# One fixed program order for TensorE, VectorE and ScalarE of a DeltaNet and Fourier-mixing kernel, with the third group begun earlier and two kinds of small products on four PE tiles

## Chip, cores and metric

The kernel runs on one core of one Trainium2 chip. The metric is device time in microseconds (us) of one execution, as the median of several. Spans in the profile are some 2 us shorter than the timed values.

## The reference, cut to what matters

```python
# DeltaNet: 4 batches, 8 heads, 768 positions, head size 48
k_n = k / (norm(k) + 1e-6)
for t in range(768):
    y[t]  = q[t] @ state                       # state is 48 x 48 for each head
    v_old = state^T @ k_n[t]
    state = state + beta[t] * outer(k_n[t], v[t] - v_old)
x = y as (4, 768, 384)
# Fourier mixing and MLP
u  = x + real(fft(fft(x, axis=1), axis=2))
un = (u - mean(u)) / sqrt(var(u) + 1e-6)
out = u + relu(un @ w1) @ w2                   # w1: 384 x 1536, w2: 1536 x 384
```

## The kernel before

The scan over positions is done in chunks of 64, so a batch is 12 **steps** and the whole scan is 48 (steps 0 to 47). Each step multiplies with a small inverse matrix that depends only on the keys. These inverses are made for two quads of four chunks at a time, which is called a **group** (six in all): VectorE inverts blocks of 32 (`invert`, tiles X and A), TensorE joins them (`merge`, tile pj) and ScalarE copies the result to `wt`. Once a batch is scanned, it is mixed (`fourier`) and goes through the MLP (tiles ph and po) in three groups of 256 rows.

Instructions that go through the wrapper keep the program's order on their engine while a flag is set. All others may be moved on their engine by the scheduler that builds the program. (PE is TensorE in the profile, DVE is VectorE, ACT is ScalarE.) In the kernel before, the flag is set in batch 0 and during the preparation of the third group's keys, and is off otherwise:

```python
    strict = [False]

    class Ordered:
        def __init__(self, engine):
            self.engine = engine

        def __getattr__(self, name):
            def call(*args, **kwargs):
                ins = getattr(self.engine, name)(*args, **kwargs)
                if strict[0]:
                    tc.keep_in_program_order(ins)
                return ins
            return call

    dve, act, pe = Ordered(nc.vector), Ordered(nc.scalar), Ordered(nc.tensor)
```

One step of the scan is a chain over three engines:

```python
    def chain(m):
        # ... cut: buffers; pc is a PSUM tile
        for j in range(2):                                   # pc <- st, KQT: 16 products in the profile
            for hh, e in ((0, 0), (1, 1), (0, 1), (1, 0)):
                pr = slice(64 * e, 64 * e + D)
                mm(pk[64 * hh:64 * hh + 64, e, j], KQT[pr, c, j, hh, 0, :], st[pr, hh, D * j:D * j + D], True)
        dve.tensor_tensor(U.rearrange(ue, e=2), V4[:, c].rearrange(ue, e=2), pk, op=ALU.subtract)
        yield
        for u in range(4):                                   # pc <- U, wt: 16 products in the profile
            for hh in range(2):
                pr = slice(64 * hh, 64 * hh + 64)
                mm(pu[pr, u], wt[pr, c, u], U[pr, u], True)
        act.activation(U, pu, ACT.Copy)
        yield
        # ... cut: loads
        for j in range(2):                                   # pc <- U, kp: 16 products in the profile
            for hh, e in ((0, 0), (1, 1), (0, 1), (1, 0)):
                pr = slice(64 * hh, 64 * hh + 64)
                mm(pS[64 * e:64 * e + 64, hh, D * j:D * j + D], kp[pr, c, 2 * j + e, :], U[pr, 2 * j + e], True)
        dve.tensor_tensor(nst, st, pS, op=ALU.add)           # the next step's state
        # ... cut: outputs (py) are left to later
        yield
```

In batch 0 the program itself says what stands between the steps' products. Afterwards it only issues preparation (`pre`) and mixing with MLP (`side`) at a rate per third of a step, and the scheduler places them:

```python
    strict[0] = True
    # ... cut: batch 0, steps 0 to 11, with the merges of groups 0 and 1 and the first weight's conversion
    run(rest)
    strict[0] = False

    PRE, SIDE = 2.4, (0.0, 1.5, 2.2, 2.2)
    pre, side, due = ahead(2), iter(()), [0.0, 0.0]
    for m in range(NCH, STEPS):
        b, n = divmod(m, NCH)
        g = m // (2 * QT)
        if m % (2 * QT) == 0:
            run(pre)                                   # a group's merge is complete before its first step
            pre = ahead(g + 1) if g + 1 < NG else iter(())
            due = [0.0, 0.0]
        for i, _ in enumerate(chain(m)):
            # ... cut: outputs; at a batch's first step, side = second(b - 1): mixing, then MLP
            if m > NCH or i > 0:
                due[0] += 4.6 if g == 1 else PRE
                due[1] += SIDE[b]
            # ... cut: advance side and pre as they fall due
```

## Time and profile before

| | before |
|---|---|
| time, median of 3 runs | 786.97 us (786.54 to 793.07) |
| span of the profiled execution | 784.7 us |
| TensorE marked busy | 699.9 us |
| mean granted clock | 0.97 |
| first product of step 12 (batch 1 begins) | 142.3 us |
| first ph (the MLP begins) | 180.3 us |
| first product of step 17 | 255.8 us |

Steps are found in the trace by their first product, `pc<-st,KQT`; a program that counts these gives the times of the table. The prediction below shows the main lines of this profile. Two more rows of its page are needed later: VectorE's busy tenths and the granted clock, in 40 slices of the span.

```profile
DVE  2699766575992598245961119783111146100000
PEclk9999999989998999699999999899999999999999
```

### The profile page before, as it was taken

What the parts mean: (1) busy time and instruction counts of PE and PEld (TensorE: products, weight loads), DVE (VectorE), ACT (ScalarE), POOL (GpSimd) and SP (SyncE); (2) the same over time, 40 slices, a digit from 0 to 9 for tenths busy, and PEclk for the clock granted to TensorE, in tenths of its full rate; (3) what the DMA queues carried; (4) which work ended last, traced back from release to release, by engine and by line L of the source; (5) the groups of instructions that cost most, each with busy time, mean ns of one, the idle gap of its engine ahead of it and who ended that gap; (6) DMA issues with size and microseconds to landing.
All of it is one profiled execution on the core that took longest, in us unless ns stands there. A gap on an engine that the chain in (4) does not pass through costs nothing.

```text
span 784.7 us, 17842 instructions
## 1 busy us (share of the span) xinstructions
PE 699.9 (89%) x7640; PEld 513.0 (65%) x7640; DVE 379.4 (48%) x952; ACT 260.0 (33%) x634; POOL 58.7 (7%) x83
## 2 busy tenths in 40 slices
PE   5852799989988997999989998999999989999997
PEld 4531687867656765786666775776767666677684
DVE  2699766575992598245961119783111146100000
ACT  3741354227436404532152540315312121021120
POOL 8020000010000001010100001010000010100000
PEclk9999999989998999699999999899999999999999
DMA  8651033225320212001202101001000000000000
GB/s 189 163 113 31 7 85 57 46 74 123 87 69 9 38 32 43 16 10 25 50 6 42 32 2 42 1 1 32 12 12 11 12 11 1 20 1 20 11 11 20
DMA packets 82447, 30.75 MB, mean 39 GB/s; under 512 B 77392, under 2 KB 78928, under 8 KB 82368
## 3 DMA queue, kind: packets, MB, share of 16 engines
q1 hardware_dynamic: 78224, 22.31, 13.8%
q0 software_dynamic: 1968, 6.91, 2.7%
q8 instruction: 60, 0.98, 0.5%
q10 hardware_dynamic: 2176, 0.39, 0.3%
q14 instruction: 19, 0.16, 0.1%
HBM read 24.87 MB, written 4.72 MB: 38 GB/s over the span
## 4 chain that ended last, share of the span: by engine, by line
PE 48%; DVE 10%; ACT 5%; issue 3%; DMA 0%; SPq 0%; POOL 0%; POOLq 0%; DVEq 0%; ACTq 0%
PE ph L131 20%; PE po L131 15%; DVE X L131 3%; PE pc L131 3%; DVE A L131 2%; PE pf L131 2%; PE pj L131 2%; ACT A L131 2%; PE pb L131 2%; ACT wt L131 1%; PE pg L131 1%; PE py L131 1%; DVE sm L131 1%; DVE x L131 1%; PE pt L131 1%
## 5 line engine op out<-in xcount | busy, mean ns | idle before, releaser
L131 PE MATMUL ph<-unT,w 128*128 128x256 f32 x864 | 213.8, 395 | 4.5 <-ACT unT L131 2.0
L131 PE MATMUL po<-w,hT 128*128 128x384 f32 x576 | 202.2, 498 | 1.7 <-ACT KQT L131 0.7
L131 PEld LDWEIGHTS ph<-unT,w 128*128 128x128 f32 x864 | 160.3, 193 | 33.7 <-ACT hT L131 3.7
L131 PEld LDWEIGHTS po<-w,hT 128*128 128x128 f32 x576 | 105.7, 191 | 68.2 <-issue 1.5
L131 ACT ACTIVATE hT<-ph 128x256 f32<-128x256 f32 x144 | 54.9, 383 | 179.6 <-PE ph L131 179.3
L131 DVE TENSOR_TENSOR x<-x,po 128x384 f32<-128x384 f32 x24 | 13.2, 552 | 112.5 <-PE po L131 112.4
L131 ACT ACTIVATE U<-pc 128x192 f32<-128x192 f32 x48 | 15.9, 331 | 110.0 <-PE pc L131 98.4
L131 ACT ACTIVATE KQT<-pt 128x256 f32<-128x256 f32 (+1 forms) x82 | 32.0, 419 | 44.9 <-PE pt L131 44.3
L131 PEld LDWEIGHTS pc<-U,wt 64*64 64x64 f32 x768 | 34.0, 163 | 19.7 <-issue 10.3
L131 PE MATMUL pg<-KQT 48*64 48x64 f32 (+1 forms) x1024 | 41.7, 309 | 5.5 <-ACT KQT L131 4.4
L131 PEld LDWEIGHTS pg<-KQT 48*64 48x64 f32 x1024 | 32.1, 178 | 20.4 <-ACT KQT L131 11.2
L131 PE MATMUL pc<-U,wt 64*64 64x48 f32 x768 | 41.2, 253 | 4.7 <-DVE U L131 2.1
L131 DVE TENSOR_TENSOR st<-st,pc 128x192 f32<-128x192 f32 x44 | 15.3, 347 | 61.0 <-PE pc L131 56.8
L131 DVE TENSOR_TENSOR U<-V,pc 128x192 f32<-128x192 f32 x48 | 16.8, 350 | 53.1 <-PE pc L131 52.9
L131 DVE TENSOR_TENSOR A<-X 128x30 f32<-128x30 f32 (+14 forms) x120 | 41.0, 342 | 2.9
L131 DVE TENSOR_TENSOR X<-X,A 128x30 f32<-128x30 f32 (+14 forms) x120 | 39.5, 329 | 2.9
L131 DVE TENSOR_TENSOR x<-x,pb 128x193 f32<-128x193 f32 (+1 forms) x96 | 26.4, 346 | 23.1 <-PE pb L131 23.1
L716 POOL DMA_INDIRECT out_dram<-x,rows_hi x12 | 12.3, 1024 | 335.9 <-DVE x L131 179.9
L131 PE MATMUL pt<-pack,kp 128*128 128x128 f32 x96 | 24.4, 349 | 10.3 <-DMA pack<-k_pack 4.8
L131 PE MATMUL pt<-pack,qp 128*128 128x128 f32 x96 | 23.4, 341 | 11.0 <-DMA qp<-in_q_dram 11.0
L131 PE MATMUL pj<-Z,A 32*64 32x64 f32 x320 | 15.0, 257 | 19.9 <-DVE Z L131 19.6
L131 ACT ACTIVATE A<-pg 128x256 f32<-128x256 f32 (+1 forms) x72 | 25.4, 378 | 21.7 <-PE pg L131 16.6
(125 smaller groups left out, 840.2 us busy)
## 6 DMA issues: line engine op xcount, KB each, us to landing
qp<-in_q_dram SPq DMA_DIRECT2D x96, 48.0 KB, 2.4
V<-in_v_dram SPq DMA_DIRECT2D x96, 48.0 KB, 2.4
kp<-in_k_dram SPq DMA_DIRECT2D x80, 48.0 KB, 2.5
w<-in_moe_w_ch_dram SPq DMA_DIRECT2D x8, 384.0 KB, 3.2
w<-in_moe_w_ch_dram POOLq DMA_DIRECT2D x6, 384.0 KB, 6.4
x<-in_moe_w_ch_dram SPq DMA_DIRECT2D x6, 384.0 KB, 3.7
x<-in_moe_w_ch_dram POOLq DMA_DIRECT2D x4, 384.0 KB, 9.2
out_dram<-x SPq DMA_DIRECT2D x8, 192.0 KB, 2.0
```

Source lines behind the costliest of these rows:

```text
L131: ins = getattr(self.engine, name)(*args, **kwargs)
L716: nc.gpsimd.indirect_dma_start(out=out.rearrange("b s m -> (b s) m"), out_offset=bass.IndirectOffsetOnAxis(ap=rows_hi[:, i:i + 1], axis=0) ...
```

## The change

The intent is to decide the whole order by hand. The flag that keeps program order is never cleared any more, on TensorE, VectorE and ScalarE. The MLP of all four batches becomes one stream of pieces (`mlps`) that are put between the products of the steps, at a fixed rate. The third group's inverse and merge stand between and behind steps 12 to 15, placed by hand. The two next quads' keys are prepared in batch 0. The adds of the mixing are done for two rows of tiles at once (six instructions in place of eight). The products `pc<-U,wt` read one half of the partitions and write the other in half of the cases, so that they use four PE tiles and not two (a PE tile is counted here as one combination of half read and half written; 16 such products took 1.09 us before and take 0.68 us after, both early in the run); so do the joining products pj of groups 2 to 5 (`crossed`), whose results then need twice as many, smaller copies by ScalarE.

```diff
     strict[0] = True
     # batch 0 ...
+    next_keys = keys(4, 5)
+    key_work = {(7, 0): 2, (8, 2): 3, (9, 0): 1, (10, 2): 2, (11, 0): 1, (11, 1): 2, (11, 2): 1}
+    first_mixing = fourier(0)
     run(rest)
-    strict[0] = False
-    PRE, SIDE = 2.4, (0.0, 1.5, 2.2, 2.2)
+    # steps 12 to 15 with the first mixing, the second weight and the third inverse, in an order by hand
+    for i in range(9):
+        next(channels)
+        advance(w, 3)
+        if i % 2 == 1:
+            advance(steps)
+        else:
+            advance(between)
+    run(w)
+    i = 0
+    while advance(inverse, 2):
+        next(channels)
+        i += 1
+        advance(between if i > 3 else steps)
+    run(between, steps)
+    for _ in merge(2):
+        next(channels)
+    pre, mixing, due = ahead(2), iter(()), [0.0] * 3
+    for m in range(NCH + QT, STEPS):
+        for i, _ in enumerate(chain(m)):
+            due = [d + r for d, r in zip(due, (1.05 if m < 2 * NCH + 4 else 2.05, 4.0, 1.1))]
+            # advance channels (MLP), pre and mixing as they fall due
```
```diff
-        for u in range(4):
-            for hh in range(2):
-                pr = slice(64 * hh, 64 * hh + 64)
-                mm(pu[pr, u], wt[pr, c, u], U[pr, u], True)
+        for j in range(2):
+            for e in range(2):
+                for hh in range(2):
+                    pr = slice(64 * (hh ^ e), 64 * (hh ^ e) + 64)
+                    mm(pu[64 * hh:64 * hh + 64, e, j], wt[pr, c, 2 * j + e], U[pr, 2 * j + e], True)
```
```diff
+            add(x[T][:, :, 0:HD + 1], pb[:, None, 0:HD + 1].broadcast_to([128, 2, HD + 1]), ALU.add)
+            add(x[T][:, :, HD + 1:DM], pb[:, None, HD - 1:0:-1].broadcast_to([128, 2, HD - 1]), ALU.add)
             for t, op in enumerate((ALU.subtract, ALU.add)):
-                add(x[T][:, t, 0:HD + 1], pb[:, 0:HD + 1], ALU.add)
-                add(x[T][:, t, HD + 1:DM], pb[:, HD - 1:0:-1], ALU.add)
```

Cut: the first merge in halves with the first state early, values and lengths stored for the crossed layout, the first mixing's folds begun in step 10.

## The prediction

> **What bounds the kernel now.** I read the page first, then the busy time by stretches of the span, then the timeline of single stretches.
>
> ```profile
> span 784.7 us, 17842 instructions
> PE 699.9 (89%) x7640; PEld 513.0 (65%) x7640; DVE 379.4 (48%) x952; ACT 260.0 (33%) x634; POOL 58.7 (7%) x83
> PE   5852799989988997999989998999999989999997
> L131 PE MATMUL ph<-unT,w 128*128 128x256 f32 x864 | 213.8, 395 | 4.5 <-ACT unT L131 2.0
> L131 PE MATMUL po<-w,hT 128*128 128x384 f32 x576 | 202.2, 498 | 1.7 <-ACT KQT L131 0.7
> ```
>
> TensorE is marked busy 89%, but that does not mean 89% used[...]. So I priced the work by its spacing where TensorE runs back to back. In the chain that ended last the end of the kernel reads:
>
> ```profile
> 683.35 15.82 PE ph L131 x72
> 700.18 15.63 PE po L131 x48
> ```
>
> One group of 256 rows of the MLP costs 31 us; the 12 groups cost 12 x 31.2 = 375 us and nothing in the change makes them cheaper. The timeline gives the small products, early (before any MLP) and late (between MLP products):
>
> ```profile
> 102.08 0.68 PE L131 MATMUL pc<-st,KQT 48*64 48x48 f32 x16
> 104.26 1.11 PE L131 MATMUL pj<-w 32*64 32x64 f32 x16
> 112.18 1.09 PE L131 MATMUL pc<-U,wt 64*64 64x48 f32 x16
> ...
> 423.92 1.15 PE L131 MATMUL pj<-Z,A 32*64 32x64 f32 x32
> 436.51 0.49 PE L131 MATMUL pc<-U,wt 64*64 64x48 f32 x10
> 589.24 0.45 PE L131 MATMUL pc<-st,KQT 48*64 48x48 f32 x16
> ```
>
> Two things are to be seen. The same 16 products take 0.68 us early and 0.45 late[...]. And the products with wt, and pj, take 1.6 times what the products with KQT take, although they are as many: they use two PE tiles, the others four. Late prices per instruction, from start to next start: pc 17 ns, pc with wt 30, py 21.5, pj 34, pg 28, pt 110, pf 100, pb 165, ptr 100, ph 216, po 325. Now the stretches:
>
> ```profile
> 0.00:88.30 88.30, 47.95 (x696) 33.97 (x696) 62.37 (x122) 37.88 (x91) 20.63 (x35) 1.00 0.50 110
> 88.30:142.30 54.00, 49.25 (x1077) 42.83 (x1075) 35.44 (x75) 25.07 (x59) 0.00 (x0) 1.00 0.29 60
> 142.30:180.30 38.00, 32.39 (x468) 27.01 (x468) 26.11 (x80) 12.13 (x28) 5.00 (x8) 0.91 0.27 61
> 180.30:255.00 74.70, 66.72 (x538) 48.12 (x542) 48.58 (x123) 40.00 (x98) 2.65 (x2) 0.93 0.30 72
> 255.00:391.00 136.00, 126.75 (x1639) 91.02 (x1636) 87.75 (x241) 46.16 (x117) 10.17 (x12) 0.92 0.16 31
> 391.00:632.00 241.00, 234.85 (x2592) 167.20 (x2594) 93.47 (x241) 72.86 (x180) 10.92 (x13) 0.99 0.07 17
> 632.00:784.70 152.70, 142.03 (x644) 102.83 (x644) 25.68 (x73) 25.94 (x63) 9.30 (x13) 0.99 0.04 12
> ```
>
> (Columns: length, busy PE, PEld, DVE, ACT, POOL, clock, DMA.) To 88: first keys and inverse, bound by VectorE and loads. 88 to 142: the 12 steps of batch 0, 4.5 us each, a chain PE, DVE, PE, ACT, PE, DVE. 142 to 180: first Fourier mixing, VectorE. 180 to 255: the MLP has started, but the scan stands still at step 16 (its first product started at 188.3, step 17's at 255.8), because the third group's inverse runs from 193 to 241 and its merge to 254; the MLP alone does not fill TensorE either. By the late prices 180 to 391 holds 157 us of TensorE work in 211 us, 391 to 779 holds 350 in 388, that is 0.90; the stretch 572 to 632 without mixing 0.93. **So TensorE bounds the kernel from about 390 on, and before that, from 180 on, some 54 us are lost to its waits for VectorE.**
>
> [...] U and wt read and wrote the same half (two tiles); the new layout crosses halves. The trace agrees that it matters: 1.09 against 0.68 us. [...]
>
> **The change, part by part.** I compared the built order of both kernels, engine by engine.
>
> *U on four tiles.* 48 steps x 16 products. Early 1.09 - 0.68 = 0.41 us a step on the chain: 12 x 0.41 = 4.9 us. Late 16 x (30 - 17) ns = 0.2 us; 32 steps: 6.6 us of TensorE time. pj of groups 3 to 5 on four tiles: 384 products x (34 - 20) = 5.4 us. ScalarE pays about 100 more small copies (some 30 us in 500, beside others; it is 33% busy): off the path.
>
> *First merge in halves, first state early.* The first product with wt comes at 89.6 now, its pj at 80.7. With half a merge between, about 87: 2.5 us.
>
> *Batch 0.* Step 12 at 142.3 - 2.5 - 4.9 = 135; keys of two quads (about 5 us of TensorE) and two of three folds (about 3 us of VectorE) now lie in steps 7 to 11, mostly in waits; I add 2: **137**.
>
> *Mixing.* From step 12 to the first ph, VectorE in its new order does: state and U 2.1, last fold and both sets of sums 6, transpose of A 2.0, norms 4.3 with ScalarE's root, scaling X 1.8, four inverse updates 1.5, sums of pb 2 x 2.5, statistics 1.5, un 1, and three U or st 1.0. With joints 28 us, so ph starts at **165** instead of 180. Adding by pairs makes six adds of eight, two of twice the width: about 0.3 us each of 12 times, 3 us of VectorE.
>
> *Third group early.* VectorE after that: rest of mixing 7, second weight 12 x (0.55 + 0.36 + 0.56) less overlap = 16, queries, U, un 4; then 28 pairs A, X at 2 x 0.375 = 21, masks and others 4; Y and two transposes 5. That is 57: inverse done at 222. Merge took 239 to 254 before and keeps its 8 stages with an MLP piece between each: 14. So the scan goes on at **236**, not 255, and the built order has 38 MLP pieces (25 a group, so 1.5 groups) done by then, 1.28 groups before.
>
> *The rest, one stream.* From 255 on the kernel before had 452 us of TensorE work. Less 9 for MLP done, plus 8 for two quads prepared later instead of before, less 12 for the tiles: **440 us**. The MLP is metered: 1.05 pieces a third of a step, so 3.15 x 1.25 = 4 us a step to step 27 and 7.7 after. I counted whether the stream starves: batch 0's 75 pieces end at step 28, the second mixing by step 28.6; batch 1's 150 at step 40, the third mixing at 40.5. It fits narrowly. The tail after step 47 is 101 pieces, as long as before.
>
> At the 0.90 of 391 to 779 before, 440 take 489 us. I take 0.89 since three mixings, not two, fall in it, and in steps 18 to 30 VectorE (32 us an inverse, 24 a mixing, 1.4 a step) is about as loaded as TensorE, so that in strict order each waits for the other at times: 494. End: 236 + 494 + 6 (last store) = 736 in the profile; the loaded time is 2 longer, and I trust the order to be tuned by a few us more than my sums: **732 us**, 7% less.
>
> **Rivals.**
> 1. *Head-of-line waits eat the gain.* With one program order, an item late on VectorE (a 2 us transpose, 2.5 us of pb adds holding one of two PSUM buffers) stops the next MLP piece, which the scheduler's order would have moved. [...] Against it: pieces of 1.25 us stand between dependent products, and 88 to 142 was strict already. With an efficiency of 0.83 the rest takes 530 and the time is 772, the edge of "same".
> 2. *Nothing but latency is lost, and the order hides it.* If the rest reaches 0.95 (MLP alone has 0.98), 463: 705 us.
> 3. *The early part does not move*, as VectorE's sum from 137 to 236 is simply delayed by the keys and folds added earlier: step 16 goes on at 250 as before; then some 746.
>
> **Range and chances.** The centre is 732; rivals 2 and 3 bound what I think likely, and half of rival 1 gives 752: 704 to 764. For a gain under 2% (771) rival 1 has to come whole: 0.06; slower needs an order worse than the old one in the saturated part too: 0.02; faster 0.92.
>
> **What would show it right or wrong.** Right: 16 products pc with wt at about 0.68 us early and 0.28 of spacing late; step 12 near 137, first ph near 165, step 17 near 238 instead of 256; no step like 16 that stands for 67 us; steps 16 to 27 about 9 us each, 28 to 47 about 12; the tail after the last step 145 to 150. Wrong: waits of ph or po for DVE x (pb adds) or ACT hT summing to over 30 us; VectorE's share in steps 18 to 30 near full while PE idles; first ph still near 180.

## The result, and the profile after

The changed kernel is **slower**: 886.41 us median of 4 runs (884.92 to 888.84), against 787.52 us (786.54 to 793.07) for the kernel before, run in the same rounds. The ratio is 1.1244, with a 95% interval of 1.1194 to 1.1294. Here and below, a ratio is the mean time of one kernel's fast runs over that of the other's in the same rounds, so it is not quite the ratio of the medians quoted. The prediction, 732 us, missed by 154.

These are rows of the page of the kernel after, to be held against those of before: the span and busy times, then the busy tenths of TensorE and VectorE and the granted clock in 40 slices.

```profile
span 883.1 us, 18294 instructions
...
PE 708.9 (80%) x7768; PEld 504.8 (57%) x7768; DVE 399.3 (45%) x972; ACT 270.5 (31%) x732; POOL 58.9 (7%) x92
...
PE   6662886767877776786677998776999989999997
...
DVE  2798767756761395143972214772522124300000
...
PEclk9999999987899977999777998788999999999999
```

TensorE's busy time grew by only 9 us, while the span grew by 98. So most of it is idle time of TensorE: from the seventh to the twenty-eighth slice, where the row of before has almost only eights and nines, it now has mostly sixes and sevens, and the recorded clock is lower there too (12 of these 22 slices read 7 or 8; in the row of before, four read below 9). VectorE is full in two of these slices only. No engine is full there, so the time goes into waits between engines. The idle time of TensorE after 86 us, added up over its gaps by a program, is 126.6 us; in before it is 35.4.

The stretches of the kernel after, cut at its own steps (first product of steps 0 and 12, first ph, steps 17, 28 and 47), show where it is lost. Columns as in the prediction: start and end, length, busy PE, PEld, DVE, ACT and POOL with their counts, granted clock, DMA share and rate.

```profile
86.50:155.20 68.70, 54.82 (x1239) 46.16 (x1237) 50.84 (x112) 31.08 (x87) 5.72 (x10) 1.00 0.26 57
155.20:182.40 27.20, 18.38 (x294) 15.54 (x294) 21.89 (x63) 5.83 (x13) 2.89 (x6) 0.94 0.10 17
182.40:287.50 105.10, 82.07 (x748) 56.51 (x748) 55.42 (x133) 45.09 (x123) 2.74 (x4) 0.90 0.23 60
287.50:437.20 149.70, 110.59 (x1472) 74.20 (x1472) 78.62 (x206) 45.03 (x127) 7.02 (x9) 0.86 0.15 28
437.20:712.70 275.50, 238.21 (x2603) 166.69 (x2603) 105.85 (x268) 82.43 (x233) 12.27 (x16) 0.90 0.06 15
712.70:883.10 170.40, 157.43 (x743) 112.28 (x742) 27.72 (x72) 25.56 (x63) 9.54 (x13) 0.99 0.04 12
```

Against the prediction's milestones: step 12 at 155.2 (137 predicted), the first ph at 182.4 (165), step 17 at 287.5 (238), the end of the last po at 877.0 (730). In the last stretch, where the MLP is nearly alone, little is lost: 170.4 us, against 168.4 in the freed kernel below.

What the waits look like is best seen at one place. The timeline of TensorE in the kernel after, during the fourth group's preparation (start, length, engine, line, operation, out<-in, shapes, count, and in brackets the idle time before it with its releaser):

```profile
303.25 0.40 PE L131 MATMUL pc<-U,kp 64*64 64x48 f32 x16
303.58 1.56 PE L131 MATMUL po<-w,hT 128*128 128x384 f32 x4
311.51 0.68 PE L131 MATMUL pc<-st,KQT 48*64 48x48 f32 x16 [6.37 <-DVE st L131]
311.97 0.64 PE L131 MATMUL py<-U,LQ 64*64 64x48 f32 x16
312.54 2.93 PE L131 MATMUL po<-w,hT 128*128 128x384 f32 x4
315.44 0.55 PE L131 MATMUL pc<-U,wt 64*64 64x48 f32 x16
315.82 0.40 PE L131 MATMUL py<-U,LQ 64*64 64x48 f32 x16
316.16 1.56 PE L131 MATMUL po<-w,hT 128*128 128x384 f32 x4
```

And VectorE at the same time:

```profile
304.98 0.69 DVE L131 TENSOR_TENSOR LQ<-pg,pack 128x512 f32<-128x512 f32 x1 [2.81 <-ACT A L131]
305.59 1.89 DVE L131 STREAM_TRANSPOSE X<-A 128x1024 f32<-128x1024 f32 x1
...
311.00 0.19 DVE L131 TENSOR_TENSOR sm<-sm,bblk 128x32 f32<-128x32 f32 x1
311.11 0.35 DVE L131 TENSOR_TENSOR st<-st,pc 128x192 f32<-128x192 f32 x1
```

The operand of `st` is ready at about 303.7, when the products `pc<-U,kp` end. VectorE is idle then and stays so to 304.98: next in its order is the mask of LQ, which waits for ScalarE. The transpose and thirteen small instructions of the inverse follow, because the program issued them before `st`. So `st` runs 7 us late: this is what the fixed order does at one place. The same is seen on TensorE: the MLP pieces at 312.54 and 316.16 need nothing from `st`, but stand behind the product that does, so TensorE is idle for 6.37 us. And the first piece after the gap takes 2.93 us, where the same four products before it took 1.56; the granted clock was 0.50 from 309.0 to 315.7, and 1.00 from 303.0 to 308.8. Here each of the two fixed orders has a share in the loss: VectorE's makes `st` late, and TensorE's holds back the MLP pieces meanwhile.

### The profile page after: what moved, and what is told of

The parts are those of the page before. It is cut to its first block, busy times and chain, and to the rows that moved or that the text cites. A ratio compares the mean times of both kernels' runs of the same rounds, so it can differ in the third digit from the quotient of the medians.

```text
span 883.1 us, 18294 instructions
## 1 busy us (share of the span) xinstructions
PE 708.9 (80%) x7768; PEld 504.8 (57%) x7768; DVE 399.3 (45%) x972; ACT 270.5 (31%) x732; POOL 58.9 (7%) x92
## 4 chain that ended last, share of the span: by engine, by line
PE 53%; DVE 23%; ACT 11%; DMA 4%; issue 4%; SPq 3%; POOL 1%; POOLq 0%; ACTq 0%; DVEq 0%
PE ph L131 18%; PE po L131 17%; PE pc L131 5%; DVE A L131 5%; DVE X L131 4%; ACT wt L131 4%; ACT A L131 3%; DVE w L131 3%; PE py L131 2%; PE pf L131 2%; SPq L218 2%; DVE x L131 2%; PE pj L131 2%; PE pg L131 2%; PE pt L131 2%
## 5 line engine op out<-in xcount | busy, mean ns | idle before, releaser
L131 PE MATMUL ph<-unT,w 128*128 128x256 f32 x864 | 222.2, 408 | 16.6 <-ACT KQT L131 7.1
L131 PE MATMUL po<-w,hT 128*128 128x384 f32 x576 | 218.5, 526 | 0.7 <-ACT KQT L131 0.5
L131 PEld LDWEIGHTS ph<-unT,w 128*128 128x128 f32 x864 | 166.9, 201 | 49.0 <-ACT hT L131 7.7
L131 PEld LDWEIGHTS po<-w,hT 128*128 128x128 f32 x576 | 110.2, 201 | 69.1 <-issue 10.5
L131 PE MATMUL pc<-st,KQT 48*64 48x48 f32 x768 | 26.5, 265 | 28.8 <-DVE st L131 28.5
L131 DVE TENSOR_TENSOR LQ<-pg,pack 128x512 f32<-128x512 f32 x16 | 11.0, 690 | 79.3 <-ACT A L131 74.7
L131 PEld LDWEIGHTS pc<-st,KQT 48*64 48x64 f32 x768 | 19.8, 169 | 45.7 <-DVE st L131 35.0
L131 DVE TENSOR_TENSOR x<-x,pb 128x191 f32<-128x191 f32 (+1 forms) x72 | 24.8, 415 | 40.9 <-PE pb L131 40.9
L131 PEld LDWEIGHTS pc<-U,wt 64*64 64x64 f32 x768 | 19.9, 164 | 23.4 <-issue 11.8
L131 PE MATMUL pj<-Z,A 32*64 32x64 f32 x320 | 10.1, 248 | 27.0 <-DVE Z L131 19.8
```

## The experiments

All fourteen kernels gave correct results. The kernel before took 785.3 to 789.4 us (medians) beside them. Times are medians of 4 runs if not said otherwise ("one run" is a single look of unknown state).

### 1. Was it the order? (a_free)

The first theory was that the fixed order itself, by waits on two engines whose order is fixed, costs most of the time. The rival was that the new amounts and places of the work do it, which a free order would not mend. The edit sets the scheduler free after batch 0 and changes nothing else of the changed kernel:

```diff
     run(rest)
+    strict[0] = False
```

> The changed kernel, but from the end of batch 0's steps on the scheduler orders all engines again, as in the kernel before; nothing else is undone. Theory O (fixed order: late items on VectorE hold back what stands behind them, TensorE idles and its clock drops): most of the 99 us come back, 765 to 800 us, and the mean granted clock returns from 0.93 to about 0.97. Theory C (what was moved and added costs by itself: keys and folds in batch 0, second weight in one block, twelve small copies a merge): 850 us or more, with the same steps standing still.

Measured: 792.41 us (792.01 to 794.7), ratio 1.0045 to before (1.0006 to 1.0084). **One line takes back 94 of the 99 us.** The same place in its trace shows how; TensorE first, then VectorE:

```profile
276.03 0.40 PE L131 MATMUL pc<-U,kp 64*64 64x48 f32 x16
276.36 1.56 PE L131 MATMUL po<-w,hT 128*128 128x384 f32 x4
277.84 0.45 PE L131 MATMUL pc<-st,KQT 48*64 48x48 f32 x16
278.11 0.41 PE L131 MATMUL py<-U,LQ 64*64 64x48 f32 x16
278.45 1.56 PE L131 MATMUL po<-w,hT 128*128 128x384 f32 x4
```
```profile
276.52 0.35 DVE L131 TENSOR_TENSOR st<-st,pc 128x192 f32<-128x192 f32 x1 [1.67 <-PE pc L131]
277.76 0.69 DVE L131 TENSOR_TENSOR LQ<-pg,pack 128x512 f32<-128x512 f32 x1 [0.89 <-ACT A L131]
278.37 1.96 DVE L131 STREAM_TRANSPOSE X<-A 128x1024 f32<-128x1024 f32 x1
```

Now `st` comes ahead of the mask and the transpose, 0.1 us after its products, and TensorE goes from one piece to the next without a gap. In the groups by line and shape, the idle time before these products (the last column, with its releasers) tells the same for the whole run. Before:

```profile
L131 PE MATMUL pc<-st,KQT 48*64 48x48 f32 x768 | 25.7, 252 | 6.2 <-DVE st L131 4.9 <-ACT U L131 0.5
L131 PE MATMUL ptr<-pack,un 128*128 128x128 f32 x72 | 12.6, 298 | 4.5 <-ACT hT L131 2.6 <-DVE x L131 1.0 <-ACT KQT L131 0.6
```

After:

```profile
L131 PE MATMUL pc<-st,KQT 48*64 48x48 f32 x768 | 26.5, 265 | 28.8 <-DVE st L131 28.5
L131 PE MATMUL ptr<-pack,un 128*128 128x128 f32 x72 | 13.9, 328 | 19.5 <-DVE un L131 18.8
```

And with the order set free:

```profile
L131 PE MATMUL pc<-st,KQT 48*64 48x48 f32 x768 | 26.3, 255 | 9.0 <-DVE st L131 8.7
L131 PE MATMUL ptr<-pack,un 128*128 128x128 f32 x72 | 13.3, 303 | 8.3 <-DVE un L131 5.4 <-DVE x L131 1.7 <-ACT hT L131 0.4
```

The times that products wait for VectorE's `st` and `un` rise from about 5 (hardly anything for `un`) to 47 us and fall back to 14. All idle time of TensorE after 86 us goes from 126.6 back to 50.5 us. So these two waits are 42 of the 91 us by which its idle time had grown; the rest is spread over many others, none of them over 12 us in total.

One thing must be kept in mind. In the freed kernel too an order was chosen before the run, by the scheduler when it built the program. What is shown is that this order by hand costs 94 us against the scheduler's, and not that every order by hand must.

### 2. Which engine's order? (a_only_pe, a_only_dve)

After batch 0, only TensorE, or only VectorE, keeps the program's order:

```diff
-            self.engine = engine
+            self.engine, self.kept = engine, engine is nc.tensor     # nc.vector in the other run
-                if strict[0]:
+                if strict[0] and (self.kept or not loose[0]):
 ...
     run(rest)
+    loose[0] = True
```

> As a_free, but TensorE keeps the program's order to the end; VectorE and ScalarE are free. If the wait is made by VectorE's order (an item ready to go behind one that isn't), then freeing VectorE alone gives back over half of what a_free gives back, about 820 us. If it is TensorE's own order that meters MLP pieces by scan steps, so that TensorE idles while MLP work is at hand, the time stays at 860 to 886.

Measured: 839.57 us (one run), 47 above a_free, between the two expectations.

> The changed kernel; after batch 0 VectorE alone keeps the program's order, TensorE and ScalarE are free. All kept is 886, all free 792, TensorE alone kept 840. If VectorE's order is the other half of the loss, about 840; if the loss needs TensorE's order (VectorE's only adds to it), 790 to 810.

Measured: 855.17 us (one run), 63 above a_free. **Either engine's order alone costs one half to two thirds of the 94**, and together they cost less than the sum of 47 and 63: the two losses overlap. The idle time of TensorE after 86 us is 97 us with TensorE's order alone and 99 with VectorE's. The largest wait differs: in a_only_pe it is for VectorE's `Z` (29.0 us), in a_only_dve for `st` (18.0). ScalarE's order alone was not run, and it is kept in after but in neither of these two.

### 3. Where along the scan? (a_free_late)

The order is kept through the hand-written part, to step 15, and set free from the main loop on:

```diff
+    strict[0] = False
     pre, mixing, due = ahead(2), iter(()), [0.0] * 3
```

> The changed kernel, with the scheduler's order only from step 16 on (all of second weight, third inverse and first MLP groups stay in strict order). Against a_free the changed kernel is 27 us later at the start of step 17, loses 35 more to step 28 and 29 more to step 47. If these losses add: 886 - 64 = 822 us, step 17 at about 287 as before. If the scheduler can make up the early loss later (the stream catches up): 800 or less.

Measured: 817.8 us (one run), so the order kept from step 16 on accounts for 69 of the 94, and that of steps 12 to 15 with the third group's start for 25. Its own trace agrees: step 17 begins at 284.9, nearly as late as in after (287.5; 260.8 in a_free), and from there to the end of the last po it takes 525 us, as a_free does (524; 590 in after).

### 4. Is it only the metering? (a_uncrossed, a_rate, a_i20)

A rival is that the order by hand is good but has bad amounts in it, which a few constants would mend. Three edits of the changed kernel, all with the fixed order, try that.

```diff
-        def __init__(self, g, lh, apart=False, crossed=True):
+        def __init__(self, g, lh, apart=False, crossed=False):
```

> The changed kernel in its strict order, but all merges write two PE tiles, so that each step of a merge takes four ScalarE copies, not eight. If the eight copies stand on the path of the strict order: 8 half groups x 2 steps x (8 x 0.27 - 4 x 0.375 = 0.66 us) = 11 us less, some of it lost to pj at 34 instead of 21 ns (4 us of TensorE): 876 to 880. If they lie beside other waits: 886, or more by the 4.

Measured: 877.18 us (876.03 to 878.54), 1.1146 (1.1068 to 1.1223), 9 better than after. (The runs don't overlap, 876.03 to 878.54 against 884.92 to 888.84; the intervals of the two ratios do, by a little.) ScalarE's copies of a merge show what is likely behind it. First ScalarE before, then ScalarE and TensorE after:

```profile
253.27 1.53 ACT L131 ACTIVATE wt<-pj 32x256 f32<-32x256 f32 x4 [1.18 <-PE pj L131]
```
```profile
346.86 2.21 ACT L131 ACTIVATE wt<-pj 32x128 f32<-32x128 f32 x8
```
```profile
349.12 0.69 PE L131 MATMUL pj<-Z,A 32*64 32x64 f32 x32 [3.52 <-ACT wt L131]
```

Eight copies of half the size take 2.21 us where four took 1.53, and TensorE, bound to its order, is idle for 3.52 us until they are done; they take up 2.21 of it, ScalarE's earlier work the rest. The 32 products themselves are faster (0.69 us, against 1.15 in the prediction's line of before), so the crossed layout saves 0.46 us of TensorE and adds 0.68 us of ScalarE to what the next product waits for. The prediction had put these copies "off the path".

```diff
-            due = [... (1.05 if m < 2 * NCH + 4 else 2.05, 4.0, 1.1) ...]
+            due = [... (1.05 if m < 2 * NCH + 4 else 2.05, 3.1, 1.1) ...]
```

> The changed kernel in strict order, with the preparation of the next group metered at 3.1 pieces a third of a step instead of 4. Where the inverse is dense (305 to 342) VectorE is busy 34 of 37 us and TensorE 23, at a clock of 0.77, as MLP pieces are metered by the steps that wait for VectorE. A thinner inverse should spread this: 5 to 15 us less, 871 to 881. If the group then comes late and is run in a block before its first step: 886 to 900.

Measured: 869.63 us (862.45 to 873.31), 1.1062 (1.102 to 1.1103), 17 better than after. That fits the theory that less of VectorE's work then stands before each `st`, as the preparation is spread over more steps.

```diff
         next(channels)
         advance(w, 3)
+        advance(inverse, 2)
```

> The changed kernel in strict order, with two updates of the third inverse put between the second weight's pieces, for which VectorE waits in order (it worked 20 of 29 us there). If the wait for the weight's transfers and splits is what delays step 17, VectorE does some 18 of the 28 pairs in it: step 17 at 270 to 275 instead of 287, but 9 MLP pieces (11 us) fewer are done by then; whole 870 to 880. If the delay is elsewhere: step 17 at 282 or later and 886 or more.

Measured: 893.17 us (892.07 to 895.43), 1.1355 (1.132 to 1.1389), 7 worse. The third inverse did end sooner (step 17 at 279.7 instead of 287.5), but with nine MLP pieces fewer behind it, so the 8 us were only lent: step 47 still begins 6 us earlier than in after, and from there to the last po it takes 178 us, against 164. Other ways to mix the inverse with the second weight's conversion have no run.

### 5. Two twins: all repairs, with and without the fixed order (a_strict2, a_free2)

Both kernels are the changed one with uncrossed merges, rate 3.1 and the next keys taken out of batch 0. They differ in one line, `strict[0] = False` after batch 0.

```diff
-        def __init__(self, g, lh, apart=False, crossed=True):
+        def __init__(self, g, lh, apart=False, crossed=False):
-    key_work = {(7, 0): 2, (8, 2): 3, (9, 0): 1, (10, 2): 2, (11, 0): 1, (11, 1): 2, (11, 2): 1}
+    key_work = {}
     run(rest)
+    strict[0] = False                       # in a_free2 only
     advance(w)
     advance(steps)
+    run(next_keys)
-    ... 4.0 ...
+    ... 3.1 ...
```

> The changed kernel in strict order with the three repairs that helped one by one: preparation at 3.1 pieces a third (17 us less), merges on two tiles (9 less), keys out of batch 0 (3 less in the freed order). If the repairs add, 855 to 862 us; if the loss is of the order as such, no setting of the pieces comes near the kernel before, and it stays over 840. Under 810 would say that only the metering was wrong, not the fixed order.

Measured: 860.72 us (855.89 to 865.08), 1.0978 (1.095 to 1.1005).

> The same three settings in the freed order, the candidate to beat both. a_free_nokeys_unc gave 777.7 to 790.2, its runs differing with the granted clock (0.983 to 0.964). If the slower preparation matters to the scheduler as it does to the fixed order: 770 to 780. If the scheduler evens it out: 780 to 790, not to be told from the kernel before.

Measured: **776.57 us** (774.3 to 779.22, 6 runs), 0.989 (0.9867 to 0.9912). So the repairs are worth 26 us in the fixed order, but the order still costs 84 with them. These amounts are a part of the loss and not the main cause; an order by hand that differs in more than these constants was not tried. The freed twin is the best kernel: 110 us below the changed kernel and about 1.1% below the kernel before, a small gain, clear of 1. Its page:

```profile
span 775.6 us, 18208 instructions
...
PE 691.0 (89%) x7768; PEld 496.5 (64%) x7768; DVE 386.7 (50%) x972; ACT 262.3 (34%) x668; POOL 58.7 (8%) x92
```

It has as many products as the kernel after, and TensorE is busy 18 us less with them, at a mean clock of 0.972 against 0.93. The step from a_free (792.41 us) isn't divided among the three repairs.

### 6. What are the small parts worth alone? (b_pairs, b_u_pairs, b_tiles_pairs)

These are the kernel **before**, its order included, with single parts of the change added.

```diff
+            add(x[T][:, :, 0:HD + 1], pb[:, None, 0:HD + 1].broadcast_to([128, 2, HD + 1]), ALU.add)
+            add(x[T][:, :, HD + 1:DM], pb[:, None, HD - 1:0:-1].broadcast_to([128, 2, HD - 1]), ALU.add)
             for t, op in enumerate((ALU.subtract, ALU.add)):
-                add(x[T][:, t, 0:HD + 1], pb[:, 0:HD + 1], ALU.add)
-                add(x[T][:, t, HD + 1:DM], pb[:, HD - 1:0:-1], ALU.add)
```

> The kernel before with mixing by pairs alone (six adds of eight). 0.3 us less of VectorE 12 times: 784 to 787 us, hardly to be told from the kernel before.

Measured: 786.4 us (784.07 to 788.4), 0.9965 (0.9921 to 1.0009): about 3 us may be gained, but the interval includes none. In the kernel after, an add for two rows takes 546 to 555 ns, where one for a single row took 345 to 349 in before, so four adds made two take some 0.3 us less.

The second adds to that the four tiles for U (with values, lengths and diagonals stored for it) and leaves the merges uncrossed:

```diff
-                mm(pu[pr, u], wt[pr, c, u], U[pr, u], True)
+                    mm(pu[64 * hh:64 * hh + 64, e, j], wt[pr, c, 2 * j + e], U[pr, 2 * j + e], True)
```

> The kernel before and its order, with U on four tiles and mixing by pairs, merges left on two tiles, and the row norms transposed at their old place (in b_tiles_pairs step 0 came 7 us late). By the prediction's sums 4.9 + 6.6 + 3 us less: 773 to 778 if they add up on the path; 784 if only batch 0 feels it. Over 790 if the crossed halves' extra diagonal copies of each merge are what b_tiles_pairs lost its time to.

Measured: 788.19 us (784.09 to 793.3), 0.9999 (0.9915 to 1.0082). Steps 0 to 11 took 50.2 us instead of 54.0, so 3.8 of the 4.9 us predicted for U are there; but the end came no sooner, and the mean clock was 0.944 to 0.964 instead of some 0.97. The products with wt in the kernel after are as short as was predicted, early and late:

```profile
127.20 0.68 PE L131 MATMUL pc<-U,wt 64*64 64x48 f32 x16
...
696.44 0.45 PE L131 MATMUL pc<-U,wt 64*64 64x48 f32 x16
696.71 0.41 PE L131 MATMUL py<-U,LQ 64*64 64x48 f32 x16
```

The next product starts 0.27 us after the later group of 16. **The products got shorter, and the kernel did not.**

The third adds crossed merges for groups 2 to 5 and the lengths' later place in `invert`:

```diff
-        def __init__(self, g, lh, apart=False, crossed=False):
+        def __init__(self, g, lh, apart=False, crossed=True):
```

> The kernel before, with three of the change's parts and its old order: U on four PE tiles, merges of the later groups on four tiles, mixing by pairs. By the prediction's sums 4.9 us in batch 0, 6.6 and 5.4 us of TensorE later, 3 us of VectorE: 770 us if they add up, 787 if all of it lies beside other waits. Over 800 if the merges' twelve small ScalarE copies, which each merge needs before the scan goes on, cost more than the tiles give.

Measured: 800.55 us (799.91 to 800.91), 1.0138 (1.0102 to 1.0175). It is 1.4% slower than before although its batch 0 took 51.0 us instead of 54.0: step 0 began at 95.2 instead of 88.3. In b_u_pairs, which differs up to there only in the place of the lengths, it began at 88.8, so that place costs some 6 us. The rest of the run lost some more; which part of it is from the crossed copies was not separated.

### 7. The keys in batch 0 (a_free_nokeys, a_free_nokeys_unc)

The freed kernel, with the next keys after batch 0 and not in it:

```diff
+    strict[0] = False
-    key_work = {(7, 0): 2, (8, 2): 3, (9, 0): 1, (10, 2): 2, (11, 0): 1, (11, 1): 2, (11, 2): 1}
+    key_work = {}
+    run(next_keys)
```

> The freed changed kernel with the keys of the third group taken out of batch 0's strictly ordered steps (they follow at its end). In a_free step 12 starts at 150.9, in the kernel before at 142.3, although U on four tiles should have made it earlier. If the keys (and not the folds) cause this: step 12 at about 138 to 142 and the whole near 782 to 788; if what is moved out comes back later on the way to step 16: 792 again.

Measured: 789.65 us (786.62 to 790.14), 1.0022 (0.995 to 1.0093). Batch 0 takes 61.1 us where a_free's takes 64.1, so the keys cost it 3 us; little of that is left at the end. The same with uncrossed merges:

> The best of the parts so far together: scheduler's order after batch 0, keys out of batch 0, merges on two PE tiles. a_uncrossed was 9 us faster than the changed kernel; a_free_nokeys stood at 789.65. If the merges' copies lie on the path here too: 780 to 783, faster than both kernels; if the freed order hides them: 788 to 790.

Measured: its four runs took 777.68 to 790.22 us. In them the longer times of one and the same program go with the lower clocks: 777.68 us at a mean granted clock of 0.983, 784.89 at 0.974, 789.49 at 0.964, 790.22 at 0.966. Which causes which is not shown.

## Why the prediction was wrong

The prediction is a sum of four stretches, so the miss can be divided by them. Its end in the profile, 736 us, lies 147 below the measured 883. In the table, "rest" is from step 17 to the end (predicted: 736 less the 238 named for step 17). The column of a_free is what the same program takes when only the order is set free after batch 0.

| stretch | predicted | after | a_free |
|---|---|---|---|
| start to step 12 | 137 | 155.2 | 150.9 |
| step 12 to first ph | 28 | 27.2 | 27.2 |
| first ph to step 17 | 73 | 105.1 | 82.7 |
| rest | 498 | 595.6 | 530.0 |

Of the 147 us, 92 are the difference between the last two columns, which is the fixed order; 55 are missing even with a free one.

**The step that failed** is "so that in strict order each waits for the other at times: 494", the efficiency of 0.89, and with it the dismissal of rival 1. The work was sized well: at the prediction's prices (17 and 20 ns for the products moved to four tiles), the kernel after has 433 us of TensorE work from step 17 on (440 predicted). But it takes 589.5 us to the last po, which is an efficiency of **0.73**. In a_free it is 0.83, in before 0.86. So a part of the miss was in the starting value: the 0.90 was read from 391 us on, where little preparation is left, and the same kernel makes 0.86 from its step 17. Rival 1 named the mechanism ("an item late on VectorE stops the next MLP piece") with 0.83 as its worst case and gave it a chance of 0.06. Neither reason against it holds:

- *"Pieces of 1.25 us stand between dependent products."* At the place shown one piece of 1.5 us stood in a wait of 8 us. The wait isn't the length of VectorE's one instruction, but everything that the program issued before `st`, with the waits of those for ScalarE. At the rate of 4 items of preparation to a third of a step, that was a transpose, thirteen small instructions and a mask.
- *"88 to 142 was strict already."* There VectorE and TensorE have few long items besides the chain. And the same strict stretch was no longer harmless when the change put keys into it: they cost 8 us there (see below).

**First ph to step 17** is off by 32 us, 22 of them from the order. The third inverse did begin earlier (173.6 us, 204.0 before), but it ended at 251.9 (235.6 before, 222 predicted), and its merge then took until 274.4, 22 us instead of 14. The prediction took the second weight's conversion as VectorE work (16 us). In the trace it is a chain of loads, since two staging buffers alternate. VectorE's groups between 195 and 224 us of the kernel after show it, and two pieces of the chain of waits in that time:

```profile
L131 DVE SCALAR_TENSOR_TENSOR wtmp<-wtmp 128x384 int32<-128x384 int32 x12 | 6.7, 556 | 10.0 <-ACT wtmp L131 9.9
```
```profile
205.28 3.60 DMA x<-in_moe_w_ch_dram
...
209.99 3.67 DMA x<-in_moe_w_ch_dram
```

VectorE is idle for 9.9 us before the twelve conversions of this window (ScalarE's part of a conversion comes between load and VectorE) and, in its fixed order, does not go on with the inverse meanwhile; a_i20 used this time. The third group was not earlier even when freed: step 17 at 260.8 us in a_free, 255.8 before. That part of the change's intent failed with either order, and the prediction's 236 with it.

**Start to step 12** is off by 18 us. Next to nothing was allowed for the keys and folds added to batch 0 ("mostly in waits; I add 2"). In the fixed order the keys cost 8 us: step 12 begins at 155.3 in a_uncrossed and at 147.0 in a_strict2, which up to there differs only in having none. When freed they cost 3 (experiment 7). One place where the order shows: step 12's state stands behind the folds, which need the last step's outputs.

```profile
153.85 0.90 PE L131 MATMUL p<-v0m,k 32*64 32x192 f32 x4 [4.14 <-DVE v0m L131]
```

TensorE waits 4.14 us there for an operand that depends on nothing recent; in a_free step 12 comes 4.3 us earlier. Without the keys, though, it comes no earlier freed than in order (147.8 in a_free2, 147.0 in a_strict2). U on four tiles gave 3.8 of its 4.9 us. Some 9 of the 18 us were not separated; folds and the second half of the first merge, which now falls into step 0, are candidates.

**What was right**: the 28 us from step 12 to the first ph (27.2), the lengths of the products with wt (0.68 us early, 0.27 us of spacing late), and the amount of work after step 17. The 28 us is partly luck: VectorE was busy for 21.9 of them, where the prediction's items add up to 26. Rival 3 was right in that step 17 did not come earlier; that it came 32 us later than before, it did not foresee. Of the signs of "right" that speak of steps and stretches, all failed: step 15 now stands for 66.6 us, as step 16 did before (67.5), and from the last step's product with wt to the last po it takes 160 us, where 145 to 150 were named. Of the three signs named as "wrong", the first ph near 180 came true (182.4). VectorE near full while TensorE idles holds for pieces of steps 18 to 30 only: it was busy for 34.3 of the 37 us from 305 to 342, but for 78.6 of the 149.7 us from step 17 to 28. The third named the wrong tiles: the largest waits are for `st` and `un`, not for the adds of pb or hT. One sum is loose too: 736 in the profile and 2 for the timed value make 738, and the 732 takes 6 off on trust, while rivals 1 and 2 (772 and 705) stand without this.

**What stays open**: about half of batch 0's loss; why the kernel before with four tiles and crossed merges (b_tiles_pairs) loses more than its later start; and how much of the 92 us is idle time and how much the lower clock. The traces put some 76 us down to idle time (126.6 against 50.5) and 17 to longer products (708.9 us busy against 692.1), but no run sets the clock apart from the gaps. Where a_free still misses the prediction by 55 us, the efficiency of 0.83 instead of 0.89 is the largest term (the rest takes 32 us longer than predicted).

## What to carry to other kernels

Where two engines with a fixed order feed each other, judge that order by the sum of all that is queued ahead of a dependent item, with its own waits, against the ready work that the other engine has in that place; one item's length says little (here `st` ran 7 us late behind fifteen instructions, the longest of 1.89 us). When an order by hand looks better in sums of work, keep the new amounts and places, let the scheduler order them, and compare the two: here that one line was worth 94 us of 886, and 84 of 861 in the twins. And shorter products need not make a shorter kernel: here U on four tiles took 3.8 us out of batch 0, and with the adds by pairs the whole stayed at 0.9999 of before (b_u_pairs).

## What else the traces show of the hardware

- *Gaps and clock.* After a gap of 6.37 us four po products took 2.93 us at a granted clock of 0.50, and 1.56 us shortly before and after, at 1.00. After 86 us the kernel after has fifteen gaps of TensorE over 3 us (65 us together), and the kernel before none (its longest is 2.4 us); the mean granted clock was 0.925 to 0.93 in the one, and 0.968 to 0.975 in the runs of the other beside a_free, which itself had 0.955 to 0.963. That the gaps make the clock low is not shown.
- *A stretch without clock records.* In the kernel after, the 16 products pc<-st,KQT of a step take 0.68 us in the seven later steps where 0.50 is recorded and 0.45 us in the 26 later steps where 1.00 is (step 22, with 0.63 us, has both). In steps 0 to 13 they take 0.64 to 0.68 us. There the profile's views print 1.00, but the trace's first clock record begins only at 165.5 us (157.1 in before). So the clock of the early part is not known, and the mean clocks above count it as full: over the recorded part alone they are 0.913 in after and 0.961 in before.
- *Four tiles instead of two.* 16 products went from 1.09 to 0.68 us, and batch 0 from 54.0 to 50.2 us (b_u_pairs). Crossing halves also split the copies of a merge: eight took 2.21 us where four took 1.53, and leaving the crossing out of the merges made the fixed-order kernel 9 us faster (a_uncrossed).
